# Linear attention and a four-branch feed-forward on one core: batch 1's q and x turned by DMAs instead of by products, with a new order of the first steps

## The chip, the cores and the metric

The kernel runs on one core of one Trainium2 chip. The metric is the device time of one execution in microseconds (us). The profile calls the engines PE (TensorE, matrix products), DVE (VectorE), ACT (ScalarE), POOL (GpSimd) and SP (SyncE, which here only issues transfers).

## The reference

The first half is a linear attention over 8 batches, 8 heads, 576 tokens and head size 64. The second half mixes four two-layer branches over the 4608 resulting rows:

```python
q_p, k_p = phi(q), phi(k)               # phi(x) = max(x + 1, min(exp(x), 1)), in effect
kv  = einsum('bhsd,bhse->bhde', k_p, v);  z = k_p.sum(axis=2)
x   = einsum('bhsd,bhde->bhse', q_p, kv) / (einsum('bhsd,bhd->bhs', q_p, z) + 1e-6)
x   = x as [4608, 512]                  # heads side by side
p   = domain_probs / domain_probs.sum(-1)
out = sum over e of p[:, e] * (relu(x @ w1[e]) @ w2[e])   # w1: 512x1024, w2: 1024x512, 4 branches
```

## The kernel before

**Tiles.** Each batch gives 512 of its 576 tokens to a tile of its own (tiles 0 to 7, in four sub-tiles of 128 tokens, index c); the 64 left rows of all batches form a ninth tile. Heads are worked in four pairs of 128 columns. For every tile and branch the first layer is done by blocks `p1` to `p7` (and `c22`, a step of DVE alone) in two halves d, with seven products of half blocks in place of eight, of four 256-column products each; the second layer by steps `m`, of the same kind, or, for tile 0, by plain steps `y{e}.{ns}{part}`, two 512-column products each, four parts to a sub-tile. The sums of blocks that the seven-product form needs are made by `s` and `t` (of weights, DVE), `ts` (of x, POOL, DVE for tile 0) and `hs` (of the hidden layer, POOL).

**Attention of a batch b** (prefix `b1.`, `b2.` and so on, class `Batch`): loads of k, v and q by quarters; `k`, `q`: ACT writes x + 1 and exp(x); `km`, `qm`: DVE's minimum and maximum of the two; `v`: ACT's cast; `lk`, `lv`, `lq`, `lkm`, `lqm`: the same for the 64 left rows; `kv`: 40 products and two copies by ACT into `kvz`; then q has to be turned, so that its head columns lie on partitions, to be the stationary operand of `nd` (numerators and denominators, followed by DVE's reciprocal and multiplication, `norm`, into x); x has to be turned in its turn to be an operand of the first layer. The left rows go through `qTl`, `nl` and `xl`. q, after its minimum, lies in the tile `qp`, which shares its one buffer with k's `kp`; x shares `vp`'s.

From batch 2 on q and x are turned by DMA transposes issued by SP (`dma_qT` L389, one for the whole of q; `dma_xT` L520, one per pair; `dma_qTl` L397; in `nd_left` L485 for the left rows). Batch 1 alone uses PE: `pe_qT` (L424), `pe_xT` (L508), `pe_qTl` (L405) and `pe_xl` (L414) multiply by an identity into PSUM, from where ACT copies the result.

**The opening** (batch 0, class `First`): loads `lq`, `lk`, `lv` of four parts each and `lpr0` (probabilities); `ke`, `kl`, `km` for k's phi (exp, linear part, minimum), `qe`, `ql`, `qm` for q's, `vc` for v's cast, `kv0` to `kv3` (18 products each and two copies into `kvz`), `qT` (four products and a copy), `nd{g}{hf}` (eight products, then a norm), `xT{pair}{hf}` (two products and a copy), and `L{g}{hf}`, the first layer of branch 0. `LQ`, `LK`, `LV`, `KL`, `QL`, `VC`, `QT`, `KC` and `XT` name the engine that issues or does each (S for SP, A for ACT, P for POOL, V for DVE). `warm` steps are products on zeros.

**The order.** Nothing is scheduled at run time: each engine runs its instructions in the order in which the program emits them, and each waits for what it needs. `CFG["EARLY"]` writes that order out by hand, up to the first branch of tile 2: each mention of a name advances that step by one stage (for `p1.100`, tile 1, branch 0, half 0: the products at the first mention, ACT's copy at the second). What the list leaves over follows by the due times of `ATTN`, `BLK` and the other tables. All weights (`w{layer}{branch}{half}`; branch 0's first layer, `w100` to `w103`, in four quarters) and batch 1's k, v, q (`k0` to `q3`, its left rows `rk`, `rv`) are loaded by POOL's queue, converted to f16 on the way where needed; `b1.load0` to `b1.load5` and `b2.load..` are SP's loads for the batch after. `BANK` says which PSUM buffers a step uses.

```python
for name in " ".join(CFG["EARLY"]).split():
    advance(name)
```

Of the kernel before, what the change touches and what calls it, by code (L numbers as in the profile page):

```python
# [12 lines left out]
FP16 = mybir.dt.float16  # L13
# [33 lines left out]
            xl=95.55,  # L47
# [26 lines left out]
    "LQ": 'SSSS',  # L74
    "LK": 'SSSS',
    "LV": 'SSSS',
    "KL": 'VVVV',
    "VC": 'AAPA',
    "QL": 'VVPV',
    "QT": 'VVAV',  # L80
    "KC": ('VV', 'VA', 'AA', 'AV'),
    "XT": ('AA', 'VV', 'VA', 'VV'),
    "CUT": (((0, 3, 4), (0, 3, 4), (0, 4), (0, 4)), ((0, 2, 4),) * 4),
    "WARM": (14, 5, 3, 1, 2, 1, 1),
    "BANK": {'qT0': 'b', 'qT1': 'py', 'kv2': 'py', 'qT2': 'py', 'kv3': 'b', 'nd10': 'b', 'nd10+': 'py', 'nd00': 'py', 'xT20': 'b', 'nd01': 'b', 'xT00': 'b', 'xT10': 'py', 'xT30': 'py', 'nd11': 'b', 'L20': 'b', 'xT11': 'b', 'L30': 'e', 'L10': 'e', 'L11': 'e', 'L00': 'py', 'L31': 'b', 'L01': 'e', 'L21': 'py', 'b1.lk': 'py', 'b1.q1': 'py', 'b1.q3': 'b', 'b1.q0': 'py', 'b1.nd10': 'b', 'b1.qT0': 'py', 'b1.nd00': 'b', 'b1.xT0': 'b', 'b1.xT3': 'py', 'b1.qTl': 'py', 'b1.nl': 'py'},
# [37 lines left out]
def kernel(  # L123
# [154 lines left out]
    class Batch:  # L278
# [56 lines left out]
        def phi_act(self, name, i):  # L335
# [3 lines left out]
            if name == "q" and self.qp is None:  # L339
                self.qp = pa.tile([P, CM, H, D], FP16, tag="kp", bufs=1, name="qp")  # L340
# [807 lines left out]
```

## Time and profile before

| | |
|---|---|
| median of 3 runs | 491.23 us (491.13 to 491.95) |
| the profiled execution | 491.24 us, of which its span (first to last instruction) is 489.5 us |
| granted TensorE clock, mean | 0.998 |
| PE busy in the span | 477.5 us |
| first product of a first layer (L654) | 18.74 us |
| first product of tile 1 (`p1.10x`) | 66.40 us |
| end of the last weight transfer (`w231`, issued at 68.3) | 76.5 us |

A row of busy time gives for a stage the microseconds in which each engine worked and, in brackets, its instructions; PEld is PE's load of the stationary operand, which runs beside the products. A waits row says which engine and line waited for which, the total, how many times, and the longest. Matrix products overlap, so what one costs is read from the distance between starts, not from its duration. A transfer's landing is counted from the start of its issue.

### The profile page before, as it was taken

To read this page: it belongs to the slowest core of one execution; us is meant where nothing else is said; L and a number is where in the kernel's file an instruction comes from. 1 tells how busy PE (TensorE), PEld (TensorE's weight loads), DVE (VectorE), ACT (ScalarE), POOL (GpSimd) and SP (SyncE) were. 2 spreads that over 40 slices of the span, in tenths; PEclk is the share of its full clock that TensorE was granted. 3 is DMA by queue.
4 is the path that set the end of the run, shared out by engine and by line. 5 is a ranking of instruction groups with operands and counts; after the bars stand their busy time and mean duration, and the time that the engine had idled before them with its cause. 6 is when DMAs were issued, how large, how long until landed. Compare 5 with 4: busy or idle time off the path is not lost.

```text
span 489.5 us, 12007 instructions
## 1 busy us (share of the span) xinstructions
PE 477.5 (98%) x4567; PEld 407.8 (83%) x4567; DVE 382.2 (78%) x801; ACT 330.8 (68%) x656; POOL 358.3 (73%) x341
## 2 busy tenths in 40 slices
PE   7899998999999999999999999999999999999996
PEld 3676665898888988898889888988898888888885
DVE  5768999998958886788769885978687756775686
ACT  5489979855896498748884888478954565446530
POOL 4655044688967896789776976697769877987775
PEclk9999999999999999999999999999999999999999
DMA  8999968532445235524552345423131020002003
GB/s 280 199 226 262 249 127 243 154 94 47 134 154 122 50 112 190 113 60 113 171 128 65 95 144 145 92 56 119 56 76 28 5 95 1 2 0 88 2 1 86
DMA packets 81017, 53.67 MB, mean 110 GB/s; under 512 B 45152, under 2 KB 73696, under 8 KB 80960
## 3 DMA queue, kind: packets, MB, share of 16 engines
q1 hardware_dynamic: 70512, 41.05, 30.7%
q0 software_dynamic: 9888, 11.41, 12.3%
q8 instruction: 35, 0.57, 0.5%
q10 hardware_dynamic: 560, 0.46, 0.3%
q14 instruction: 22, 0.18, 0.1%
HBM read 45.16 MB, written 9.44 MB: 112 GB/s over the span
## 4 chain that ended last, share of the span: by engine, by line
PE 91%; ACT 3%; DVE 2%; DMA 1%; issue 1%; SPq 0%; DVEq 0%; ACTq 0%
PE py L809 39%; PE pb L866 24%; PE pe L866 18%; PE py L714 4%; PE ph L654 1%; PE psum_nd L471 1%; DMA kraws<-in_k_dram 1%; PE psum_kv L443 1%; DVE acc L705 1%; PE pb L809 1%; PE pe L809 0%; DVE t L761 0%; PE psum_nl L489 0%; ACT kp L343 0%; ACT u L877 0%
## 5 line engine op out<-in xcount | busy, mean ns | idle before, releaser
L705 DVE SCALAR_TENSOR_TENSOR acc<-py,p_sb,acc 128x256 f32<-128x256 f32 (+1 forms) x382 | 181.7, 488 | 43.1 <-PE py L809 37.3
L850 DVE CUSTOM_DVE_ANT_0 h<-pe,u 128x512 f16<-128x512 f32 x140 | 96.0, 687 | 46.8 <-PE pe L866 27.1
L866 PEld LDWEIGHTS <-w 128*128 128x128 f16 x1120 | 109.1, 98 | 17.4 <-issue 1.3
L776 POOL TENSOR_TENSOR hs<-h 128x512 f16<-128x512 f16 x64 | 73.9, 1154 | 59.4 <-DVE h L850 57.5
L809 PEld LDWEIGHTS <-h 128*128 128x128 f16 x1024 | 99.6, 98 | 12.7 <-issue 1.2
L809 PE MATMUL py<-w,h 128*128 128x256 f16 x744 | 106.4, 273 | 0.6 <-ACT acc L703 0.6
L877 ACT COPY u<-pb 128x512 f32<-128x512 f32 x140 | 82.5, 592 | 32.4 <-PE pb L866 29.7
L778 POOL TENSOR_TENSOR hs<-hs,h 128x512 f16<-128x512 f16 x64 | 75.0, 1173 | 26.4 <-PE py L809 24.0
L866 PEld LDWEIGHTS <-s 128*128 128x128 f16 x840 | 81.4, 98 | 12.1 <-issue 1.1
L866 PE MATMUL pb<-tt,w 128*128 128x256 f16 x560 | 83.7, 273 | 0.9 <-ACT u L877 0.9
L809 PEld LDWEIGHTS <-hs 128*128 128x128 f16 x768 | 74.4, 98 | 8.9 <-POOL hs L776 0.2
L782 POOL TENSOR_TENSOR hs<-h,hs 128x512 f16<-128x512 f16 x64 | 74.7, 1168 | 0.9 <-PE py L809 0.3
L780 POOL TENSOR_TENSOR h<-h 128x512 f16<-128x512 f16 x64 | 74.8, 1168 | 0.2
L809 PE MATMUL py<-t,hs 128*128 128x256 f16 x496 | 74.3, 273 | 0.0
L899 ACT ACTIVATE h<-pe 128x512 f16<-128x512 f32 x70 | 42.0, 600 | 44.1 <-PE pe L866 40.7
L892 ACT COPY pe<-pb 128x512 f32<-128x512 f32 x70 | 40.1, 574 | 38.6 <-PE pb L866 14.1
L920 ACT ACTIVATE h<-pb 128x512 f16<-128x512 f32 x70 | 42.0, 600 | 7.0 <-PE pb L866 7.0
L866 PE MATMUL pb<-tt,s 128*128 128x256 f16 x280 | 41.8, 272 | 0.6 <-ACT pe L892 0.6
L866 PE MATMUL pe<-tt,s 128*128 128x256 f16 x280 | 41.9, 273 | 0.0
L866 PE MATMUL pe<-xT,s 128*128 128x256 f16 x248 | 37.3, 273 | 0.0
L866 PE MATMUL pe<-xT,w 128*128 128x256 f16 x248 | 37.2, 273 | 0.0
L866 PE MATMUL pb<-xT,w 128*128 128x256 f16 x248 | 37.0, 273 | 0.0
(133 smaller groups left out, 598.7 us busy)
## 6 DMA issues: line engine op xcount, KB each, us to landing
out_dram<-acc SPq DMA_DIRECT2D x32, 256.0 KB, 2.5
w<-in_moe_w_dram POOLq DMA_DIRECT2D x14, 512.0 KB, 10.7
rawb<-in_k_dram SPq DMA_DIRECT2D x24, 256.0 KB, 3.3
rawb<-in_v_dram SPq DMA_DIRECT2D x24, 256.0 KB, 2.8
rawb<-in_q_dram SPq DMA_DIRECT2D x24, 256.0 KB, 2.7
rawq<-in_q_dram SPq DMA_DIRECT2D x4, 256.0 KB, 5.5
w<-in_moe_w_dram POOLq DMA_DIRECT2D x4, 256.0 KB, 6.1
rawb<-in_k_dram POOLq DMA_DIRECT2D x4, 256.0 KB, 8.6
```

What stands on the lines that cost most here:

```text
L705: nc.vector.scalar_tensor_tensor(out=acc, in0=ps, scalar=pscal, in1=acc, op0=AO.mult, op1=AO.add)
L776: nc.gpsimd.tensor_tensor(out=hs[0], in0=a21, in1=a22, op=AO.add)
L778: nc.gpsimd.tensor_tensor(out=hs[1], in0=hs[0], in1=a11, op=AO.subtract)
L780: nc.gpsimd.tensor_tensor(out=a21, in0=a11, in1=a21, op=AO.subtract)
L782: nc.gpsimd.tensor_tensor(out=hs[3], in0=a12, in1=hs[1], op=AO.subtract)
L809: nc.tensor.matmul(out=ps, lhsT=lhsT(k), rhs=rhs[:, k], start=first and k == 0, stop=k == FH - 1, skip_group_check=True,)
L850: nc.vector._custom_dve(TENSOR_ADD_SAT, out=out, in0=ps, in1=u, s0=BIG, s1=0.0)
L866: nc.tensor.matmul(out=ps[:, kk], lhsT=lk(kc), rhs=rhs[:, kc], start=first and kk == 0 and kc == 0, stop=kc == 1, skip_group_check=True,)
L877: nc.scalar.copy(u, self.b)
L892: nc.scalar.copy(self.e5, self.b)
L899: nc.scalar.activation(self.h[:, :, 0, 0:NH], self.e5, AF.Relu)
L920: nc.scalar.activation(self.h[:, :, 1, 0:NH], self.b, AF.Relu)
```

## The change

Batch 1's q is turned by four DMA transposes issued by SP, one for each pair (`b1.qT0` to `b1.qT3`), its x by four (`b1.xT0` to `b1.xT3`), its left rows by two for q and two for x, as in the other batches. The four functions with products go. For this q is laid out pair-major, `[P, NPAIR, CM, P]`, in all batches from 1 on, so that one pair is a contiguous piece. The list `EARLY` is a new order of nearly all steps to the same depth, a few steps longer; the twelve loads of the opening are spread over SP, ACT and POOL, some of the opening's steps change engines, and the products on zeros become 31 in five places instead of 27 in seven. `BANK` gets new entries (not shown). Of `EARLY` the diff shows the stretches of the opening and of batch 1's q and x.

```diff
             xt=(48.15, 50.45, 51.45, 54.8),
             qtl=57.23,
             nl=71.0,
-            xl=95.55,
             next=(-0.5, 0.5, 36.3, 44.55, 46.65, 47.45),
...
-    "LQ": 'SSSS',
-    "LK": 'SSSS',
-    "LV": 'SSSS',
-    "KL": 'VVVV',
-    "VC": 'AAPA',
-    "QL": 'VVPV',
-    "QT": 'VVAV',
-    "KC": ('VV', 'VA', 'AA', 'AV'),
-    "XT": ('AA', 'VV', 'VA', 'VV'),
+    "LQ": 'SSAP',
+    "LK": 'AASS',
+    "LV": 'PSSP',
+    "KL": 'VPVV',
+    "VC": 'AAVA',
+    "QL": 'VVVP',
+    "QT": 'VAAA',
+    "KC": ('AA', 'VA', 'AA', 'VV'),
+    "XT": ('AV', 'AA', 'VV', 'AV'),
     "CUT": (((0, 3, 4), (0, 3, 4), (0, 4), (0, 4)), ((0, 2, 4),) * 4),
-    "WARM": (14, 5, 3, 1, 2, 1, 1),
+    "WARM": (18, 8, 1, 2, 2),
     "EARLY": (
-        "lq0 lk3 lk1 ql0 qe0 lq2 ke1 ql2 kl1 w103 qe2 ke3 kl3 lv1 w100 lk0 lq1 km1 qm0 ke0 kl0 w102 w101 km3 warm0 qT0 ql1 lv0 qm2 km0 vc1 vc0 w111 lq3 ql3 qT0",
-        "warm1 kv1 kv1 lk2 qe3 lv2 vc2 kv1 qT2 qT2 lv3 rk1 kv0 w110 ke2 qe1 kv0 kv0 qm3 vc3 kl2 warm2 nd01 nd00 warm3 qT3 v0 nd00 w200 nd01 warm4 xT10 kv3 xT11",
...
-        "c22.020 b1.k1 p5.021 y1.11 p7.021 p7.021 w131 b1.km1 b1.k0 p4.020 p3.020 y1.20 y1.21 q0 b1.k2 p4.020 p4.021 c22.021 p3.020 b1.load5 p3.021 b1.km0",
-        "y1.12 b1.v3 p4.021 b1.km2 b1.load0 y1.13 b1.kv b1.kv p3.021 y1.22 y1.23 b1.q3 y1.30 y1.13 y1.23 q1 y1.31 y1.32 y1.33 b1.q2 p1.031",
-        "p1.031 y1.00 p1.030 p1.030 b1.qm3 y1.33 b1.qT3 b1.qm2 y1.01 b1.qT2 s3.0 s3.1 p2.030 y1.02 b1.qT3 b1.nd30 y1.03 s3.3 b1.qT2 b1.nd21 b1.loadlq p6.030",
-        "b1.load2 lpr w220 p2.030 b1.nd30 w221 b1.q1 y1.03 p6.030 p5.030 b1.qm1 b1.nd31 p2.031 p7.030 b1.q0 b1.nd31 p6.031 b1.qm0 b1.next y2.00 p7.030 y2.01",
-        "p4.030 p2.031 b1.qT1 p6.031 p4.030 b1.nd21 w230 b1.qT0 b1.nd20 p7.031 c22.030 p5.031 b1.qT0 b1.nd00 b1.xT3 s3.2 b1.nd20 b1.nd01 b1.qT1 p3.030 b1.xT2",
-        "b1.nd00 b1.nd10 b1.nd01 y2.20 b1.xT3 b1.nd11 y2.21 b2.ones p7.031 b1.xT2 b1.lq b1.xT0 y2.22 y2.23 b1.xT0 b1.nd10 b1.nd11 b1.xT1 b1.xT1 b2.load1 y2.02",
...
+        "lk1 lv1 ke1 lq3 qe3 lk3 kl1 kl3 lk0 ql3 lpr0 pr0 qm3 vc1 km1 lv2 lq2 lq0 lv0 ke3 km3 lk2 qe0 lq1 qe1 kl2 warm0 kv1 vc2 lv3 w101 w103 ke2 kl0 ke0 km2",
+        "k0 warm1 kv2 vc0 km0 warm2 kv0 ql1 qm1 kv2 qT1 vc3 ql0 qm0 kv1 kv0 qT1 kv2 kv3 kv1 w100 kv3 qT3 qT0 kv3 nd10 w102 qe2 ql2 qT3 qT0 kv0 warm3 nd00 w110",
+        "nd10 qm2 nd11 qT2 qT2 xT20 w111 nd00 warm4 xT10 xT30 rk0 xT20 xT00 xT10 nd01 nd11 xT30 w200 nd01 xT31 xT21 xT00 L10 L10 xT11 L10 xT21 xT01 xT01 w201",
...
+        "p6.020 y0.33 p2.020 b1.k1 y0.33 p2.021 p7.020 y0.23 b1.km3 s0.2 v2 p5.020 p7.020 w211 y1.10 q2 q1 w130 p6.021 y1.00 p2.021 y1.01 p6.021 p5.021 b1.lv",
+        "p7.021 s2.2 p7.021 b1.lkm b1.v2 c22.020 p3.020 b1.v0 q0 y1.11 c22.021 b1.v3 p4.020 p4.020 b1.km1 b1.q1 y1.02 w131 y1.03 t1.0 b1.kv p4.021 y1.12 p4.021",
+        "y1.13 y1.30 b1.kv p3.021 p1.030 p1.030 y1.31 w220 b1.q2 y1.32 y1.03 y1.20 b1.qm1 b1.q0 p1.031 p1.031 p3.020 y1.21 y1.22 y1.33 y1.13 y1.23 t1.1 p3.021",
+        "q3 b1.qT1 b1.qm2 p2.031 w221 s3.0 s3.1 p2.030 p2.030 y1.33 p6.030 s3.3 p6.031 p6.030 p5.030 p6.031 b1.qm0 b1.nd10 p7.030 p7.030 b1.q3 p7.031 y1.23",
+        "b1.nd10 s3.2 b1.qT2 c22.030 y2.10 p2.031 b1.qT0 y2.20 p4.030 y2.21 b1.qm3 b1.qT3 t0.3 b1.nd21 p3.030 t2.0 b1.nd11 y2.11 b1.nd21 b1.nd11 p5.031 y2.22",
+        "y2.23 y2.12 p7.031 c22.031 b1.nd20 y2.13 p3.031 y2.23 y2.13 b1.nd01 b1.nd00 b1.nd00 y2.00 p4.030 y2.01 y2.02 b1.nd01 b1.nd20 y2.03 y2.30 y2.31 p4.031",
+        "p4.031 b1.nd30 b1.xT1 b1.load1 b1.xT0 y2.03 b1.load0 w230 b1.nd31 b2.k1 y2.32 y2.33 p3.030 b1.xT2 b1.nd31 b1.nd30 b1.xT3 y2.33 b1.loadlq y3.00",
+        "b1.load2 y3.01 t3.0 w231 y3.02 b1.load4 b2.k0 y3.20 y3.03 p3.031 p1.100 y3.03 p1.100 ts1.0 p1.101 p1.101 ts1.1 y3.21 y3.30 t0.1 y3.31 b2.load0 t1.3",
+        "p2.100 p2.101 b2.km0 p2.100 p2.101 b1.lq y3.22 t2.1 b2.load1 p6.100 p6.101 p6.100 p6.101 ts1.2 y3.32 t3.1 t2.3 p5.100 b2.v1 p7.100 p7.100 b2.v0",
+        "b2.ones b2.km1 y3.23 p7.101 b2.v2 c22.100 y3.33 y3.33 p7.101 ts1.3 p4.100 p5.101 b1.load5 p4.100 p3.100 y3.10 b1.load3 p4.101 c22.101 b2.k3 y3.03",
...
@@ -337,9 +336,12 @@
             if name == "k" and self.kp is None:
                 self.kp = pa.tile([P, CM, H, D], FP16, tag="kp", bufs=1, name="kp")
             if name == "q" and self.qp is None:
-                self.qp = pa.tile([P, CM, H, D], FP16, tag="kp", bufs=1, name="qp")
+                self.qp = pa.tile([P, NPAIR, CM, P], FP16, tag="kp", bufs=1, name="qp")
             src = self.raw[name, i]
-            dst = (self.qp if name == "q" else self.kp)[:, :, i * HQ : (i + 1) * HQ, :]
+            if name == "q":
+                dst = self.qp[:, i].rearrange("p c (h d) -> p c h d", h=HQ)
+            else:
+                dst = self.kp[:, :, i * HQ : (i + 1) * HQ, :]
             nc.scalar.activation(dst.rearrange("p c h d -> p h c d"), src, AF.Identity, bias=1.0)
             ee = aps([P, HQ * CM * D], FP32, "psum_ee")
             ee = ee.rearrange("p (c h d) -> p c h d", c=CM, h=HQ)
@@ -386,12 +388,13 @@
                     out=dst, in0=dst, scalar=1.0, in1=el[us], op0=AO.max, op1=AO.min
                 )
 
-        def dma_qT(self):
+        def dma_qT(self, i0=0, n=NPAIR):
             if self.qT is None:
-                self.qT = pa.tile([P, CM, NPAIR, P], FP16, tag="qT", bufs=1, name="qT")
+                self.qT = pa.tile([P, NPAIR, CM, P], FP16, tag="qT", bufs=1, name="qT")
+            pairs = slice(i0, i0 + n)
             nc.sync.dma_start_transpose(
-                out=self.qT.rearrange("p c a i -> p (c a) i"),
-                in_=self.qp.rearrange("p c h d -> p (c h d)"),
+                out=self.qT[:, pairs].rearrange("p a c i -> p (a c) i"),
+                in_=self.qp[:, pairs].rearrange("p a c i -> p (a c i)"),
             )
 
         def dma_qTl(self):
@@ -401,36 +404,6 @@
                     out=self.qTl[:, :, u, us],
                     in_=self.ql[us].rearrange("p h d -> p (h d)"),
                 )
-
-        def pe_qTl(self):
-            ps = aps([P, 2, P], FP16, "psum_ql")
-            for a in range(2):
-                nc.tensor.transpose(out=ps[:, a], in_=self.ql[:, 2 * a : 2 * a + 2], identity=identh)
-            yield
-            for u in range(2):
-                us = slice(u * HP, (u + 1) * HP)
-                nc.scalar.copy(out=self.qTl[:, :, u, us], in_=ps[:, :, us])
-
-        def pe_xl(self):
-            ps = aps([P, 2, P], FP16, "psum_xl")
-            for a in range(2):
-                nc.tensor.transpose(out=ps[:, a], in_=self.xl[:, a], identity=identh)
-            yield
-            c0 = self.b * SL
-            for u in range(2):
-                us = slice(u * HP, (u + 1) * HP)
-                nc.scalar.copy(out=xT_left[:, 2 * u : 2 * u + 2, c0 : c0 + SL], in_=ps[:, :, us])
-
-        def pe_qT(self, pair, eng=nc.vector):
-            ps = aps([P, CM, P], FP16, "psum_qT")
-            for c in range(CM):
-                nc.tensor.transpose(
-                    out=ps[:, c], in_=self.qp[:, c, 2 * pair : 2 * pair + 2], identity=identh
-                )
-            yield
-            if self.qT is None:
-                self.qT = pa.tile([P, CM, NPAIR, P], FP16, tag="qT", bufs=1, name="qT")
-            (eng.copy if eng is nc.scalar else eng.tensor_copy)(out=self.qT[:, :, pair], in_=ps)
 
         def kv(self):
             ps = aps([P, NPAIR, DE], FP32, "psum_kv")
@@ -470,7 +443,7 @@
                 pair, c = divmod(i0 + i, CM)
                 nc.tensor.matmul(
                     out=ps[:, i],
-                    lhsT=self.qT[:, c, pair],
+                    lhsT=self.qT[:, pair, c],
                     rhs=self.kvz[:, pair],
                     start=True,
                     stop=True,
@@ -497,25 +470,13 @@
             self.xl = pa.tile([P, 2, P], FP16, tag="xsl", bufs=1, name="x_sl")
             self.norm(self.xl, ps, 2)
             yield
-            for u in range(2) if self.b != 1 else ():
+            for u in range(2):
                 us = slice(u * HP, (u + 1) * HP)
                 c0 = self.b * SL
                 nc.sync.dma_start_transpose(
                     out=xT_left[:, 2 * u : 2 * u + 2, c0 : c0 + SL],
                     in_=self.xl[us].rearrange("p a i -> p (a i)"),
                 )
-
-        def pe_xT(self, pair):
-            ps = aps([P, CM, P], FP16, "psum_xT")
-            for c in range(CM):
-                nc.tensor.transpose(out=ps[:, c], in_=self.x[:, pair, c], identity=identh)
-            yield
-            if self.xT is None:
-                self.new_xT()
-            nc.scalar.copy(
-                out=self.xT[:, pair],
-                in_=ps.rearrange("p c i -> p (c i)"),
-            )
 
         def dma_xT(self, pair):
             if self.xT is None:
@@ -972,12 +933,12 @@
         if not first:
             put(at["lqd"] + 2, f"b{b}.qTl", bt.dma_qTl)
         if first:
-            put(at["qtl"], f"b{b}.qTl", bt.pe_qTl)
+            put(at["qtl"], f"b{b}.qTl", bt.dma_qTl)
             for i in range(NPAIR):
-                put(at["qt"][i], f"b{b}.qT{i}", bt.pe_qT, i, nc.scalar)
+                put(at["qt"][i], f"b{b}.qT{i}", bt.dma_qT, i, 1)
                 for hf in range(2):
                     put(at["nd"][i], f"b{b}.nd{i}{hf}", bt.nd, i * CM + 2 * hf, 2)
-                put(at["xt"][i], f"b{b}.xT{i}", bt.pe_xT, i)
+                put(at["xt"][i], f"b{b}.xT{i}", bt.dma_xT, i)
             for i in range(NRAW):
                 put(at["next"][i], f"b{b}.load{i}", load, len(mine) + i)
         else:
@@ -985,8 +946,6 @@
             for i in range(6):
                 put(at["nd"][i], f"b{b}.nd{i}", numerators, 3 * i, min(3, NPAIR * CM - 3 * i))
         put(at["nl"], f"b{b}.nl", bt.nd_left)
-        if first:
-            put(at["xl"], f"b{b}.xl", bt.pe_xl)
 
     def warm(n):
 
```

## The prediction

> **What bounds the kernel now.** I read the page's part 1 first, then the busy time by stages, who TensorE (PE) waited for, the queues by tile, and the timeline.
>
> ```profile
> PE 477.5 (98%) x4567; PEld 407.8 (83%) x4567; DVE 382.2 (78%) x801; ACT 330.8 (68%) x656; POOL 358.3 (73%) x341
> ```
>
> PE is the bound on average. The stages say where it is not alone:
>
> ```profile
> core 0: us, PE busy (x) PEld busy (x) DVE busy (x) ACT busy (x) POOL busy (x), PEclk, DMA share, GB/s
> 0.00:15.00 15.00, 11.17 (x90) 5.01 (x91) 9.62 (x24) 8.81 (x14) 8.56 (x18) 1.00 0.94 261
> 50.00:60.00 10.00, 10.00 (x84) 6.73 (x80) 8.82 (x18) 9.47 (x20) 0.00 (x0) 1.00 1.17 255
> 75.00:80.00 5.00, 4.12 (x31) 2.77 (x30) 4.93 (x11) 5.00 (x11) 0.26 (x1) 1.00 0.66 214
> 80.00:85.00 5.00, 4.35 (x65) 2.93 (x64) 4.96 (x8) 4.25 (x9) 4.84 (x4) 1.00 0.85 253
> 100.00:110.00 10.00, 10.00 (x100) 9.01 (x99) 9.39 (x22) 6.27 (x13) 8.20 (x7) 1.00 0.38 91
> ```
>
> To 15 us the loads bind. From 50 to 60, where batch 1's q is turned, PE, VectorE (DVE), ScalarE (ACT) and the DMA engines are all nearly full. From 75 to 85 DVE and ACT are full and PE loses 1.53 us. After that it is PE alone. PE's waits from 20.6 us to 450 us, all of them:
>
> ```profile
> PE pb L866 <- ACT u L877: 0.9, 1, 0.9
> PE pb L866 <- ACT pe L892: 0.6, 1, 0.6
> PE py L809 <- ACT acc L703: 0.6, 1, 0.6
> ```
>
> So 2.1 us is all that a better order can win there; more needs less PE work or an earlier start.
>
> **The products and copies removed.** Two lines of PE's timeline price them:
>
> ```profile
> 54.05 0.39 PE L427 MATMUL psum_qT<-identh,qp 128*128 128x128 f16 x4
> 54.27 0.59 PE L714 MATMUL py<-w,h 128*128 128x512 f16 x2
> ```
>
> Four products hold PE for 54.27 - 54.05 = 0.22 us. Gone are 16 for q, 16 for x, 2 and 2 for the left rows: 36 x 0.055 = 1.98 us, in a stretch where PE is full: **-2.0**. Gone with them are ACT's copies, 4 x 0.60, 4 x 0.585 and 4 x 0.27 = 5.8 us, the last two at 123 us; ACT is not the end of the chain there, but two of PE's three waits (1.5 us) are waits for ACT at 75 to 85 us, a few us behind these copies. DVE is full there as well, so I take 1.0 of the 1.5: **-1.0** (bounds 0 and -1.5).
>
> The pair-major layout of q leaves ACT's and DVE's instructions at the same elements (0.63 and 0.68 us rows): 0. The four more warming products are 4 x 0.21 us in PE's opening idle time (3.8 us to 15 us): 0; without that cover, 0.9.
>
> **The opening.** Before, SP issues all twelve loads, one per 0.5 us; from the fifth on they land every 0.7 us, the last (v, pair 3) at 7.3 + 6.2 = 13.5. That is 288 KB per 0.73 us: rate, not issuing, sets it, so three queues win little. Against it, the new order puts k's pair 1 and q's part 3 on GpSimd (POOL) ahead of the loads of v's pairs 0 and 3. POOL's one such step took 2.14 us. Chain: k1 lands at some 4.2 (the first load took 2.8, its own landing before was 6.5); POOL's k step 2.14 x 576/512 = 2.4, to 6.6; q step to 8.75; issue of v0 0.7, of v3 0.7 from 9.45. Its landing takes between 2.8 (the first load) and 7.1 (w101's, same queue, same crowd); I take 4.3, near the 13.5 by which the same bytes were in before: 13.75. From there to the first layer-1 product: cast, products and kvz copies 1.65; q step and qT copy 0.75; norm of nd10 0.95; qm2 0.35; norm of nd00 0.9; three ACT copies of xT 1.55: 6.2, so 19.95. By then 5.86 us of useful products are done (rows of 0.11 to 0.6 us summed along the new order). Before, the dense stretch starts at 20.64 with 6.74 done. (19.95 - 5.86) - (20.64 - 6.74) = **+0.2**, bounds -1.3 and +3.0 from the landing. ACT's loads of k0 and q2 stand behind its waits for k1 and q3, and are issued at about 6 to 8; k0 then lands at 9.5 to 12, needed by kv0 at 13.4: covered.
>
> **Batch 1 by DMAs.** The transposes that the trace has, all after 86 us:
>
> ```profile
> L523 SPq DMA_TRANSPOSE xT<-x_sb x24: 1188/1216/1380, 105.7 to 366.8; - x24
> ...
> DMA to landing us min/median/max: 2.3/2.3/3.3
> ```
>
> Those are the same 128x512 tiles. But the q ones would now run at 50 to 63 us beside the weight stream. Two rows for that crowd: SP's load of 256 KB issued at 46.23, and the packets between 52 and 60 us:
>
> ```profile
> rawb<-in_k_dram SPq DMA_DIRECT2D x1, 256.0 KB, 7.4
> ```
>
> ```profile
> q0 software_dynamic: 1104, 1.19, 81.7%
> q1 hardware_dynamic: 1105, 0.67, 37.0%
> ```
>
> The two queues got one packet each in turn, 69 pairs per engine in 8 us: 0.116 us a pair. Two stretches with one transpose each (105.5 to 107.4, 109.9 to 112.0 us) show 480 and 651 packets, 35 per engine for each, in 1.2 us of DMA time together: 35 x 0.116 = 4.1 us instead of 0.6 on the engines, so about 2.3 + 3.5 = 5.8 in the crowd. Bounds: 2.3 (alone) and 11.7 (the 256 KB load issued at 49.8 behind others); I take 5.8, as the new order has no loads on SP just ahead of q's.
>
> Whether that is hidden is the distance from issue to use. PE at place x of the new list is at x + 7.45 us (19.95 for place 12.5). b1.kv ends at 48.9; b1.q1 (whose buffer is kp's, so ACT waits there for kv, 2 us, with p4.021's ReLU, kvz and p1.030's copy behind it, none needed before 51) gives 50.0, DVE's minimum 50.7, so qT1 is issued at 50.8 and first used by nd10 at 49.7 + 7.45 = 57.1: 6.3 us. Likewise qT2 5.8, qT0 6.3, qT3 6.3. At 5.8 all are just covered: 0. At 7.4 PE waits 1.1 once (a wait gives the later ones the same time), at 11.7 it waits 5.4.
>
> The Trainium skill (DMA: Bandwidth & Descriptors, Queues, rings and completion order) says each DMA engine takes turns between queue rows packet by packet. The 1104 against 1105 agrees; by the rule alone the sum stays at the covered case, and only the 7.4 row speaks for a wait.
>
> For x the order goes norm, transpose, tile 1's first products. DVE from 50 us has minima, weight sums, accumulations, norms and ReLUs back to back: those from b1.qm1 to b1.nd30's norm sum to 19.5 us at 0.56 to 0.67 each, while PE's list from 50.0 to that place holds 18.0. So DVE ends 1.5 us late, and on the way its ReLU c22.031 is done at 63.7 where p3.031 is due at 63.2, and y2.23's accumulation at 64.4 where y2.00 needs its bank at 63.9, 0.5 each. Between 0.5 and 1.5 I take **+1.2**, bounds 0 (DVE runs ahead in the lighter list before 50 us) and 2.0. After that wait xT0 is issued at 66.4 for p1.100 at 71.4, xT3 at 69.7 for p2.100 at 73.5: 5.0 and 3.9 us, against 2.3 to 3.3 once the weights are in, at 67 to 68 (w230 landed at 46.5 + 17.8 = 64.3 before; w231, issued at 68.3 then, now follows it at once, and y3.02 needs it at 70.1). SP's loads of batch 2 stand between: load1 behind xT1, issued at 64, lands in 3.4 to 7.6; ACT's b2.k1 behind it is at 68.3, so ACT may wait up to 3, with p1.100's copy at 71.8 behind it: covered. The stream itself: the four q and first x transposes hold the DMA engines 5 x 0.6 = 3.0 us, about what SP's loads at 46 to 50 us took in before, now later; w221 then lands at about 61.7, where y2.22 is due at 61.4: 0.3, inside the 1.2 too.
>
> ```profile
> 68.52 3.42 DVE L761 TENSOR_TENSOR t<-w 128x1024 f16<-128x1024 f16 x1
> 69.10 1.17 POOL L847 TENSOR_TENSOR tt<-xT,tt 128x512 f16<-128x512 f16 x1
> 70.22 1.16 POOL L847 TENSOR_TENSOR tt<-xT 128x512 f16<-128x512 f16 x1
> ```
>
> This f16 step takes 0.68 elsewhere; beside POOL's token sums it took 3.42, so 2.7 lost. The new order has five such steps among the four sums, so the loss is there again, 0.68 to 4.6 us of DVE; it is why I don't take all 1.5 above.
>
> **The sum.** -2.0 - 1.0 + 0.2 + 1.2 = -1.6 on the profiled execution's 491.24 (span 489.5 and 1.74 around it, equal to the runs' median of 491.23): 489.6.
>
> **Rivals.** *All hidden*: DVE's lateness falls into slack and ACT's 1.5 is won: -2.0 - 1.5 + 0.2 = 487.9. For it: the 6.3 us distances, and 2.1 us of waits in 430 us now. Against: DVE's 8.82 of 10.
>
> *DVE takes it back*: the change takes nothing from DVE, so PE's 2.0 turns into waits for DVE at 50 to 85 us, +1.2 and 0.8 more, ACT's 1.0 stays lost: 491.24 - 2.0 + 0.2 + 2.0 = 491.4. For it: DVE 4.93 of 5 at 75. Against: its whole load to there is the same in both orders.
>
> The Trainium skill (SBUF — State Buffer, Terms) says of the port pair that DVE and GpSimd share that the loser fully blocks for an instruction. The 3.42 us step agrees, and this rule speaks for that rival.
>
> *Slower, q's transposes starve*: at a landing of over 6.3 us nd10 stands still, PE with it, as no product behind nd10 may pass. At the 9.9 of SP's load issued at 48.9, PE waits 3.6, which includes DVE's 1.2: 491.24 - 2.0 - 1.0 + 0.2 + 3.6 = 492.0; at 11.7 it is 493.8. It decides from 9.1 (a wait of 2.8 undoes the gain). For it: every SP transfer of 46 to 51 us took 7.4 to 14.1. Against: those queued behind each other. I set 492.9.
>
> *Slower, a late opening*: v3 landing after 7.1 instead of 4.3, +2.8: 492.4.
>
> **Numbers.** Forecast 0.33 (489.6), all hidden 0.13, DVE takes it back 0.16, starving 0.25, late opening 0.13. The measurement tells 0.2%, 1.0 us, from no change; so faster 0.46, same 0.16, slower 0.38. The forecast's own range is 488.5 to 490.2; 8 in 10 lie within 487.7 and 493.8.
>
> **What would show it.** Right: no L427, L511, L408, L417 rows; twelve more DMA transposes, q's landing in about 5.8; the first L654 product near 20; PE waits under 1.5 us between 50 and 70 us, put down to DVE, and fewer than 1.5 at 75 to 85. Wrong: PE or its weight load at nd's line waiting for a DMA into qT, L866 waiting for one into xT, L714 for weights, or a first L654 after 21.5.

## The result and the profile after

The changed kernel takes 496.11 us (median of 6 runs, 494.92 to 497.23) against 491.2 us for the kernel before on the same chip (6 runs, 490.71 to 491.95): 1.0099 of its time, 95% interval 1.0082 to 1.0116. It is 4.9 us slower; forecast were 489.6 us, and 487.7 to 493.8 us as the range for 8 in 10. One execution is left out of the times below: in the first run of x alone by DMAs with SP's queue free, one of four took 507.85 us at a granted clock of 0.943, the others 495.74 to 497.61 at 0.986 or more. The profiled execution of after took 496.26 us with a span of 494.5 us, at a granted clock of 1.0.

The first part of the profile's page, of after:

```profile
PE 476.6 (96%) x4535; PEld 406.2 (82%) x4535; DVE 379.1 (77%) x797; ACT 326.9 (66%) x648; POOL 361.1 (73%) x344
```

PE works 0.9 us less (477.5 before) in a span that is 5.0 us longer, so some 5.9 us of new idle time have to be found. The busy time by stages finds them (after, PE alone; the columns are the length of the stage, PE's busy time and instructions, the granted clock, the DMA engines' share and GB/s):

```profile
20.60:50.00 29.40, 29.05 (x256) 1.00 1.19 237
50.00:70.00 20.00, 16.74 (x115) 1.00 1.22 197
70.00:85.00 15.00, 14.83 (x101) 1.00 0.73 186
85.00:130.00 45.00, 40.79 (x404) 1.00 0.54 145
130.00:450.00 320.00, 320.00 (x3144) 1.00 0.34 88
```

The two stages of before that count most here:

```profile
50.00:70.00 20.00, 20.00 (x173) 1.00 0.92 182
85.00:130.00 45.00, 44.98 (x410) 1.00 0.42 110
```

Idle in the five stages is 0.35, 3.26, 0.17, 4.21 and 0 us; before it was 0.12, 0, 1.53, 0.02 and 0.57. So there are two losses: 3.3 us at 50 to 70 us, where batch 1's q is turned, and 4.2 us at 85 to 130 us, well after batch 1's q and x are turned. What ACT cost PE at 70 to 85 us is gone, as hoped. PE's waits of after from 20 to 130 us name those who end the idle time:

```profile
PE psum_nd L444 <- DMA qT<-qp: 4.1, 4, 1.6
PE py L770 <- ACT acc L664: 1.4, 1, 1.4
PE pb L827 <- ACT h L881: 1.0, 1, 1.0
PE pb L827 <- ACT u L838: 0.7, 2, 0.4
PE pb L827 <- POOL tt L808: 0.5, 1, 0.5
```

**The first loss.** Three of the four waits for q (the fourth, 0.9 us, is batch 2's) stand in PE's timeline of after at the numerators of batch 1 (line 444; the bracket is the idle time and what ended it):

```profile
59.95 0.29 PE L444 MATMUL psum_nd<-kvz,qT 128*128 128x130 f16 x2 [1.64 <-DMA qT<-qp]
...
64.29 0.29 PE L444 MATMUL psum_nd<-kvz,qT 128*128 128x130 f16 x2 [1.45 <-DMA qT<-qp]
...
68.44 0.40 PE L444 MATMUL psum_nd<-kvz,qT 128*128 128x130 f16 x4 [0.17 <-DMA qT<-qp]
```

The tile's own view, from 48 to 75 us, gives the issue and the landing of the four transposes:

```profile
L395 SPq DMA_TRANSPOSE qT<-qp x4: 1191/1214/1318, 51.8 to 63.1; - x4
...
DMA to landing us min/median/max: 5.9/8.6/10.1
```

In order they took 8.1, 9.1, 10.1 and 5.9 us; the first three landed at 59.9, 64.2 and 68.4, one every 4.2 us. The packets of after, first from 52.9 to 54.5 us, then from 57 to 59 us:

```profile
q0 software_dynamic: 305, 0.33, 121.3%
```

```profile
q0 software_dynamic: 311, 0.32, 91.3%
q1 hardware_dynamic: 312, 0.08, 29.7%
```

Queue 0 carries the weights, queue 1 the transposes. Between them the landing falls into two parts. The first transpose is issued at 51.8 us, and its first packet leaves only at 55.7, 3.9 us later; until then the weights' queue alone sends. From there the two queues send one packet each in turn, and the transpose's 544 packets, 34 for each of 16 engines, take 3.9 us, to 59.6. In before, the transpose issued at 105.7 us with no weights beside it needed 1.2 us to its first packet (106.9) and 0.8 us for its packets.

**The second loss.** SP's queue of after (start, duration, transfer) issues for 24 of the 26.7 us from 74.6 to 101.3; before it issued for 16 us in that time:

```profile
82.92 0.61 SPq L317 DMA_DIRECT2D rawb<-in_q_dram  x1
83.69 1.35 SPq L295 DMA_DIRECT2D rl<-in_k_dram  x2
...
87.78 2.48 SPq L403 DMA_TRANSPOSE qz<-qlp  x2
...
92.49 0.48 SPq L317 DMA_DIRECT2D rawb<-in_q_dram  x1
93.53 2.44 SPq L476 DMA_TRANSPOSE xT_left<-x_sl  x2
96.10 1.12 SPq L317 DMA_DIRECT2D rawb<-in_q_dram  x1
...
98.26 2.45 SPq L403 DMA_TRANSPOSE qz<-qlp  x2
100.82 0.52 SPq L317 DMA_DIRECT2D rawb<-in_q_dram  x1
```

The four loads of batch 2's q go out at 82.9, 92.5, 96.1 and 100.8 us. Of the added transposes only four stand among them, those of the left rows at 87.8 and 93.5 us, 4.9 us of issuing; the rest is what the new list puts there. In the kernel before they went out between 77.4 and 81.8:

```profile
77.37 2.41 SPq L318 DMA_DIRECT2D rawb<-in_q_dram  x3
...
81.45 0.37 SPq L318 DMA_DIRECT2D rawb<-in_q_dram  x1
```

So ACT of after waits for one of them, PE then waits for ACT (the 1.4 us for line 664 above, which stands behind this step on ACT), and q's transpose of batch 2 is issued at 106.3 instead of 92.7 us and makes PE wait 0.9 us more:

```profile
97.77 0.63 ACT L345 ACTIVATE qp<-rawb 128x512 f16<-128x512 f32 x1 [1.39 <-DMA rawb<-in_q_dram]
```

### The profile page after: what moved, and what is told of

Same layout as the page of the kernel before. It is cut to its first block, busy times and chain, and to the rows that moved or that the text cites. A ratio compares the mean times of both kernels' runs of the same rounds, so it can differ in the third digit from the quotient of the medians.

```text
span 494.5 us, 11962 instructions
## 1 busy us (share of the span) xinstructions
PE 476.6 (96%) x4535; PEld 406.2 (82%) x4535; DVE 379.1 (77%) x797; ACT 326.9 (66%) x648; POOL 361.1 (73%) x344
## 4 chain that ended last, share of the span: by engine, by line
PE 79%; DMA 11%; DVE 4%; ACT 3%; POOL 1%; issue 1%; DVEq 0%; POOLq 0%; ACTq 0%
PE py L770 36%; PE pb L827 21%; PE pe L827 16%; DMA qT<-qp 3%; DMA rl<-in_k_dram 3%; PE py L675 2%; DMA w<-in_moe_w_dram 1%; DMA rawq<-in_q_dram 1%; PE psum_nd L444 1%; DVE acc L666 1%; DMA xT<-x_sb 1%; DMA rawb<-in_q_dram 1%; PE psum_kv L416 1%; DVE t L724 1%; ACT u L838 1%
## 5 line engine op out<-in xcount | busy, mean ns | idle before, releaser
L737 POOL TENSOR_TENSOR hs<-h 128x512 f16<-128x512 f16 x64 | 74.3, 1161 | 55.7 <-DVE h L811 47.9
L739 POOL TENSOR_TENSOR hs<-hs,h 128x512 f16<-128x512 f16 x64 | 73.9, 1155 | 25.4 <-PE py L770 22.9
L770 PEld LDWEIGHTS <-hs 128*128 128x128 f16 x768 | 74.5, 98 | 10.1 <-issue 1.7
L770 PE MATMUL py<-w,hs 128*128 128x256 f16 x248 | 36.9, 273 | 1.4 <-ACT acc L664 1.4
```

Of the source, the lines that this page charges most:

```text
L737: nc.gpsimd.tensor_tensor(out=hs[0], in0=a21, in1=a22, op=AO.add)
L739: nc.gpsimd.tensor_tensor(out=hs[1], in0=hs[0], in1=a11, op=AO.subtract)
L770: nc.tensor.matmul(out=ps, lhsT=lhsT(k), rhs=rhs[:, k], start=first and k == 0, stop=k == FH - 1, skip_group_check=True,)
```

## The experiments

Theories at the start. **A, the crowd**: q's transposes land late because the weights' stream has the DMA engines, and PE waits for them; **B, SP's queue**: the new order and 12 more transposes, 1.2 us of issuing each, hand out batch 2's loads too late. Their rival **C**: one loss is the other's lateness handed on, or the new order as such is slower. All ratios are to the kernel before on the same chip.

### Without q's transposes

```diff
 def dma_qT(self, i0=0, n=NPAIR):
+    if self.b == 1:
+        self.qT = self.qp
+        return
     nc.sync.dma_start_transpose(...)
```

> The new kernel without the four DMA transposes of batch 1's q: the numerators read q as it lies (that part of the computation is left out), so they wait only for DVE's minimum. All else, the order too, as in the new kernel. Theory (the transposes land late beside the weight stream, 8 to 10 us in the profile, and PE waits 1.64 + 1.45 + 0.17 us for them): PE's idle time from 50 to 70 us falls from 3.26 us to under 0.6; the waits of 85 to 160 us (4.0 us, ACT waiting for batch 2's q) come from the order of SP's loads and stay: 492.5 to 493.5. Rival one, the later waits only follow from the first: both go, 489.5 to 490.5. Rival two, the new order itself makes PE wait there (DVE, PSUM buffers): 495 to 496.5.

492.61 us (9 runs), ratio 1.0030 (1.0010 to 1.0050), so 3.4 us of the 4.9 went with four transposes. PE's stages:

```profile
50.00:70.00 20.00, 20.00 (x173) 1.00 0.93 177
70.00:85.00 15.00, 14.70 (x100) 1.00 0.78 205
85.00:130.00 45.00, 41.00 (x410) 1.00 0.54 137
```

The first loss is 0 and the second is still 4.0 us: it is not the first one handed on. PE is busy all of 50 to 70 us as well, so DVE's lateness, for which the prediction charged 1.2 us, costs nothing once q is there.

### One q load earlier

```diff
-... p4.110 b2.load6 p1.120 ... t3.3 b2.load4 b2.q2 ...
+... p4.110 b2.load4 p1.120 ... t3.3 b2.load6 b2.q2 ...
```

> The new kernel with two loads of SP exchanged in the list: batch 2's third quarter of q (b2.load4), which stood one step ahead of its use on ACT, takes the place of batch 3's first k (b2.load6), a dozen steps earlier. If the later loss comes from that load's place in the order: ACT's wait of 1.4 us at that quarter and PE's 1.36 us at 98 us go, with part of the 2.4 us of 110 to 160 us behind it: 493.0 to 494.8. If those waits only follow from the first loss at 58 to 68 us: 495.8 to 496.5.

496.24 us (4 runs), 1.0106 (1.0070 to 1.0143): nothing won. That time fits the second expectation, though its reason, lateness handed on from the first loss, is out by the run before. The wait at 98 us went (idle at 90 to 100 us 0.07 instead of 1.46), and came back at 100 to 120 us (2.3 instead of 0.9): the last q load now went out at 102.2 us. So one place in the queue is not the bound; whether the q loads together are is tested below.

### Half of the weight stream of 50 to 70 us left out

In both kernels, the second layer's weights of branches 2 and 3 are zeroed by POOL instead of loaded.

```diff
-            nc.gpsimd.dma_start(out=w2_sb[e][:, fs], in_=w2_src[e, :, fs])
+            if e >= 2:
+                nc.gpsimd.memset(w2_sb[e][:, fs], 0.0)
+            else:
+                nc.gpsimd.dma_start(out=w2_sb[e][:, fs], in_=w2_src[e, :, fs])
```

> The new kernel with the second-layer weights of branches 2 and 3 set to zero by GpSimd in place of their four transfers of 1 MB (read) each: that part of the computation is left out, the DMA engines have no crowd from some 50 us on. To be set against the kernel before with the same edit. If the crowd makes the transposes late: they land in 2.3 to 3.5 us, PE waits under 0.5 us at the numerators from 50 to 70 us, and this kernel is at most 1.8 us above the other (the later loss stays), or 1 to 2 us below it if the later loss follows from the first. If the transposes are slow for another reason (their small packets, the SP queue): landing stays over 6 us and the difference stays at 4 to 5 us.

> The kernel before with the same edit (second-layer weights of branches 2 and 3 zeroed by GpSimd, four transfers fewer), as the other half of the pair. It has no transposes in that stretch: 490 to 492, within 1 us of the kernel before by every theory, unless weights or GpSimd's work bound it there.

After: 492.15 us (10 runs), 1.0029 (1.0012 to 1.0045). Before: 490.22 us (10 runs), 0.9978 (0.9965 to 0.9992). The difference between the two kernels falls from 0.0099 to 0.0051, which is 2.5 us still (1.9 by the medians), a little over the 1.8 us expected. The transfers of the edited after from 50 to 70 us:

```profile
qT<-qp SPq DMA_TRANSPOSE x4, 2.4
```

Same place, same instructions: 2.4 us instead of 8.6, and PE idles 0 at 50 to 70 us. The first transpose, issued at 52.6 us, sends its first packet at 53.9, after 1.3 us and not 3.9. Theory A stands. The 4.2 us of the second loss are still there (40.80 busy of 45).

### Copies instead of transposes

```diff
+    if self.b == 1:
+        nc.sync.dma_start(out=self.qT[:, pairs], in_=self.qp[:, pairs])
+        return
     nc.sync.dma_start_transpose(...)
```

> The kernel after with batch 1's four q transposes replaced by plain copies of the same 128 KB from the same tile to the same tile in SP's queue (1 KB packets where the transposes move 256 byte ones; q arrives unturned, so the result is not the reference's). Theory P (packets): a transpose is late because each of its many small packets waits for its turn beside the weights' packets; a copy with a quarter of the packets lands in 3 to 5 us, PE doesn't wait for it, and the time is 492 to 493.5 us. Rival (the crowd alone): any transfer that starts there waits for the weight stream; it lands in 8 to 10 us as the transposes do, and the time stays at 495.5 to 497 us.

493.8 us (8 runs), 1.0054 (1.0038 to 1.0070), a little over what the packets' theory gave. The transfers from 50 to 70 us:

```profile
qT<-qp SPq DMA_DIRECT2D x4, 128.0 KB, 5.6
```

Same bytes, same crowd: 5.3 to 5.7 us, with no queueing, and PE idles 0 at 50 to 70 us. The start is as late as the transposes': the first copy is issued at 52.2 us, and from there to 56.0 the weights' queue sent 713 packets and SP's none. Then the copy's 144 packets, 9 for each engine, took 1.5 us, where the first transpose's 34 took 3.9. So the late start of 3.8 to 3.9 us meets both forms, and the transpose's many small packets cost 2.4 us more, which also makes the next one queue behind it.

### Two queues

```diff
+            eng = nc.scalar if self.b == 1 and i0 in (0, 2) else nc.sync
-            nc.sync.dma_start_transpose(
+            eng.dma_start_transpose(
```

> The kernel after, with two of batch 1's four q transposes (pairs 0 and 2) issued in ACT's DMA queue and two in SP's, as before in place and size. Theory Q (one queue's turn): the four transposes queue behind one another, 4.2 us of service each beside the weight stream, so two queues serve them side by side; PE's waits for q fall from 3.3 us to 0.5 to 1.5 us, and the time to 493.5 to 495 us (ACT loses two issues, 1.2 us each, off the critical path at that place). Rival (the engines' rate): the small packets share the DMA engines whatever queue they stand in; landings stay at 8 to 10 us, and the time at 495.5 to 497 us.

499.72 us (4 runs), 1.0174 (1.0159 to 1.0189): outside what either expected, and no test of them. The timeline of ACT's two issues:

```profile
61.24 1.29 ACTq L396 DMA_TRANSPOSE qT<-qp  x1
...
69.43 1.21 ACTq L396 DMA_TRANSPOSE qT<-qp  x1
```

SP's two were issued at 52.5 and 66.9. Each was issued only after the one before it, in the other queue, had landed (the first at 60.4), so they ran one at a time, and ACT stood still for 7.44 us around the last. Whether two queues would serve them side by side stays open.

### Batch 2's q loads first

```diff
-b2.load6 ... b3.load1 ... b2.load4 ... b2.load3 ... b2.load8 ... b2.load5
+b2.load4 ... b2.load3 ... b2.load5 ... b2.load6 ... b3.load1 ... b2.load8
```

> The kernel after, with six loads of the raw ring in another order in SP's list: the three late q loads of batch 2 (issued at 92.5, 96.1 and 100.8 us in the profile of after) take the first three of six places (91.5 to 101.4 us), the k and v loads that stood there take the last three. Theory A (the order): SP hands out the q loads too late for batch 2's q steps, and PE's 4 us of idle between 85 and 130 us follow from it; the last q load then goes out some 7 us sooner, and the time is 492.5 to 494.5 us, PE idle in 85 to 130 us below 2 us. Theory B (the slots): the ring has six slots, a load can't start before the load six ahead of it has been used, so a new order only moves the lateness to k and v; 495.5 to 497 us, idle still 3.5 us or more.

> The kernel after with both suspected causes taken away: batch 1's four q transposes left out (the numerators read q as it lies, so that the result is not the reference's), and the six ring loads with batch 2's q loads first. Two separate losses, both as named: 488.5 to 490.5 us (the kernel with q unturned took 492.6, less 2 to 4 us). If the order of the loads is not the cause of the later loss: 492 to 493.5 us as before this edit. PE idle in 50 to 70 us 0 in either case.

The order alone: 494.78 us (4 runs), 1.0066 (1.0047 to 1.0084). With q unturned: 491.68 us (10 runs), 1.0004 (0.9993 to 1.0015). Against the same kernels in the old order that is 1.6 and 1.3 us less, with PE idle at 85 to 130 us 2.0 and 2.2 us instead of 4.2 and 4.0. The first and then the second kernel:

```profile
85.00:130.00 45.00, 42.96 (x430) 1.00 0.53 140
```

```profile
85.00:130.00 45.00, 42.78 (x429) 1.00 0.52 141
```

That is just over what theory B gave (494.5 us at most, idle under 2 us), and well under the rival's 3.5 us or more of idle time: B is right for half of the second loss. (The profiled execution of the order alone, 492.89 us, is the fastest of its four.) The last q load now went out 9 us sooner, at 91.4 us instead of 100.8, but batch 2's q transpose only 2.5 us sooner, at 103.8: 12 us behind that load, where it was 5.5 us in after, so something else than the loads' issue holds it there. In the second kernel the other half is waits of 1.1 us for batch 2's q transpose, 0.6 for POOL and 0.4 for ACT; no run takes them apart. I had expected 488.5 to 490.5 us with both causes gone; 491.68 is the kernel before's own time, and the gain of the prediction's sum isn't there.

### x alone by DMAs, in the order of before; and all of it

```diff
-                put(at["xt"][i], f"b{b}.xT{i}", bt.pe_xT, i)
+                put(at["xt"][i], f"b{b}.xT{i}", bt.dma_xT, i)
...
-            put(at["qtl"], f"b{b}.qTl", bt.pe_qTl)
+            put(at["qtl"], f"b{b}.qTl", bt.dma_qTl)
```

> The kernel before with only batch 1's x, left x and left q rows turned by DMAs (20 products and their copies on ACT fewer); q turned by products as before, the opening and the list of steps as before but for the dropped second halves of these steps. If the later loss of after lies in the list's order and not in these DMAs: 488 to 490.5 us, with PE's 1.5 us of idle at 70 to 85 us gone. If the DMAs themselves cost it (SP's 13 us of added issues push batch 2's loads): 492 to 495 us, with PE idle at 90 to 130 us as in after.

> The kernel before with all of batch 1's turns by DMAs, q by head pairs, in the order and the opening of before (only the left rows of batch 2 are loaded after batch 1's left q has been read, since that load would stand ahead of two q transposes in SP's queue and wait for it). If the landing in the crowd is the first loss: the first numerators stand closer behind their transposes here (3 to 7 us) than in after, so PE waits 4 to 9 us at 50 to 70 us and the time is 493.5 to 498 us. If the new order is what makes after slower: 489 to 491.5 us.

x alone: 498.89 us (4 runs), 1.0157 (1.0133 to 1.0180). All by DMAs: 506.07 us (4 runs), 1.0311 (1.0287 to 1.0335), over even the expected range of theory A. So the new order doesn't make these DMAs dear: in the old one they cost three times as much (15.1 us against 4.9). What the new order costs or wins with products for q and x no run shows. SP and PE of the x kernel:

```profile
52.19 7.24 SPq L250 DMA_DIRECT2D praw<-in_moe_domain_probs_dram  x2
64.83 1.25 SPq L294 DMA_DIRECT2D rl<-in_k_dram  x2
...
68.82 5.24 SPq L521 DMA_TRANSPOSE xT<-x_sb  x4
```

```profile
73.98 0.37 PE L864 MATMUL pb<-xT,w 128*128 128x256 f16 x1 [6.66 <-DMA xT<-x_sb]
```

The transposes land in 2.3 us, but stand in SP's queue behind two loads of 4 KB that took 7.24 us to issue in the crowd and behind the left rows, which wait 5.1 us for ACT. Behind PE's long wait the granted clock was 0.50 from 74 to 78 us, so a part of this run's cost is the clock. From 85 to 130 us this kernel idles only 0.5 us, with eight more transposes in SP's queue than before, so these alone don't make the second loss. (The wait of 7.5 us ahead of it gave the loads time, so this is no clean proof.)

### The numerators later

```diff
-b1.nd10 p7.030 p7.030 b1.q3 p7.031 y1.23 ... t0.3 b1.nd21 p3.030 t2.0 b1.nd11 y2.11 ... y2.22 ...
+p7.030 p7.030 b1.q3 p7.031 y1.23 b1.nd10 ... t0.3 p3.030 t2.0 y2.11 ... y2.22 b1.nd21 b1.nd11 ...
-p1.100 ... p1.101 ... y3.21 y3.30
+y3.21 y3.30 p1.100 ... p1.101
```

> The kernel after with batch 1's numerator steps some 2 to 3 us of PE work later in the list (behind parts of the first tile's second layer that stood after them) and tile 1's first two steps behind four more such parts; the transposes are left as and where they are. If the first loss is only the distance between a transpose's issue and its use (landings of 8 to 10 us against 6 us in the list): PE's waits for q fall from 3.3 us to below 1 us, and the time to 493 to 495 us. If the chain behind the numerators (x, its transposes, tile 1) needs them at the old places: the wait reappears as one for xT at 70 to 80 us, and the time stays at 495.5 to 497.5 us.

> The same with the six ring loads of batch 2 in the order q first, as in the run of that order alone. If the two losses are separate, as the runs with q unturned say: 1.3 to 2 us under the run with the numerators later alone, so 491.5 to 493.5 us; the kernel before at 491.2 us is reached at best, not beaten by more than 1 us. If the second loss is only the first one's lateness handed on: no difference between the two runs.

496.11 us (4 runs), 1.0094 (1.0068 to 1.0121), and with the q loads first 494.95 us (4 runs), 1.0071 (1.0045 to 1.0096). The second is 1.1 us under the first, a little less than the 1.3 to 2 expected, and over its range of 491.5 to 493.5 us. The larger waits of the first, 20 to 130 us:

```profile
PE psum_nd L444 <- DMA qT<-qp: 1.9, 3, 1.1
PE py L770 <- ACT acc L664: 1.8, 2, 1.5
PE pb L827 <- ACT u L838: 1.7, 2, 1.6
PE py L675 <- DVE acc L666: 0.9, 2, 0.6
```

The waits for batch 1's q fell to 0.85 us, as the distance theory had it, but the time stayed, as the other had it, though not by a wait for x: 1.5 us came back as waits for DVE, 0.4 as waits for ACT, and PE's idle time from 20.6 to 130 us is 7.8 us instead of 8.0. Here moved steps only handed the lateness on.

### x alone by DMAs, with SP's queue free

q by products; SP's left rows and second probabilities behind x's transposes.

```diff
-b1.load2 lpr w220 ... b1.next y2.00 ... b1.xT1 b2.load1
+b1.load2 w220 ... y2.00 ... b1.xT1 b1.next b2.load1 ... b1.load3 lpr
```

> The kernel before with batch 1's x and left rows turned by DMAs, q by products, and SP's loads of batch 2's left rows and of the second probabilities moved behind the four x transposes (the steps that read the left rows a little later too); tile 1's first steps where they were. x's transposes then go out at 62 to 66 us and land 2.3 us later, the last near 68, while tile 1's first product is due at 65 to 66: a wait of 2 to 3 us instead of 7.5. If the x part is worth its 20 products and copies (-1.1 and up to -1.5): 490.5 to 493 us. If SP's later work is pushed into a new wait at 70 to 130 us: 494 us or more.

> The same with tile 1's first steps some 2.5 us of second-layer products later, so that x has landed. If the x part is worth its 20 products and copies: 488.5 to 490.5 us, under the kernel before. If the time freed is lost to SP's later work or to DVE: 491 to 494 us.

496.23 us (3 runs), 1.0109 (1.0075 to 1.0144), and 495.63 us (4 runs), 1.0102 (1.0046 to 1.0157). The first fits its expectation of 494 us or more; the second is over both of its own. The wait for x is gone in the second, and nothing is lost at 90 to 130 us; two others are there, and the second of them costs more than its length:

```profile
70.65 0.60 PE L864 MATMUL pb<-tt,s 128*128 128x256 f16 x4 [1.75 <-POOL tt L845]
...
79.37 0.60 PE L487 MATMUL psum_nl<-kvz,qz 128*128 128x130 f16 x4 [2.48 <-DMA qz<-qlp]
79.81 1.60 PE L712 MATMUL py<-w,h 128*128 128x512 f16 x4
```

```profile
80.00:82.00 2.00, 2.00 (x8) 0.53 0.53 53
82.00:84.00 2.00, 2.00 (x12) 0.62 0.77 220
```

A last run moved these two steps as well:

```diff
-y2.13 b1.nl y3.22 ... c22.100 b1.nl y3.23 ... b2.load9 b1.nl p4.100
+y2.13 y3.22 ... y3.10 b1.nl y3.00 y3.01 b1.nl p4.101 y3.02 b1.nl
```

> The kernel of the last run with batch 1's left numerators and norms some 5 us of products later, and tile 1's first step that reads the token sums some 2 us later. If those two waits and the clock behind them are what is left: 489.5 to 492 us, PE idle at 60 to 90 us below 1.5 us and its clock 1.0 there. If the list is so tight that the waits only move on: 493 us or more.

496.81 us (4 runs), 1.0108 (1.0080 to 1.0137). The waits moved on again: 3.09 us for DVE at 82.9, 1.41 for weights at 76.6, 1.09 for DVE at 84.4. No kernel tried here that does all of the work beats the one before.

## Why the prediction was wrong, step by step

- **The landing in the crowd, 5.8 us**, is the term that failed first. It measured 8.1 us for the first transpose, with nothing of its own queue ahead of it. The sharing that the sum added was right: 35 packets at 0.116 us a pair are 4.1 us, and 34 took 3.9 here. The Trainium skill (DMA: Bandwidth & Descriptors, Queues, rings and completion order) says that the engine takes turns packet by packet; this trace agrees where both queues have packets, with 311 to 312. What failed is the rest of the 2.3 us, which the sum kept as measured alone: the start, from the issue to the first packet, was 1.2 us there and 3.9 beside the weights. 3.9 for the start, 3.9 for the packets and the 0.3 that is left of the 2.3 make 8.1. The trace of before had it: SP's load issued at 46.23 us sent nothing until 49.8, so 3.6 of its 7.4 us were start, but the sum read that row as one number and set it aside. That the weights' stream causes the late start is shown by the run without it (1.3 us); how it holds the first packet back is not.
- **"A wait gives the later ones the same time"** failed too. It looked at each transpose alone. The first three are issued 3.3 us apart and served one every 4.2 us, so the second and third queued behind the one before, landed still later (9.1 and 10.1), and the distances of 5.8 to 6.3 us were short by more each time. PE's waits for it: 1.64 + 1.45 + 0.17 = 3.26, where the sum had 0. The rival *q's transposes starve* named mechanism, place and price: a wait of 3.6 at a landing of 9.9; without the idle time of the next point the account below comes to 492.1 us, against its 492.0.
- **SP's loads behind x's transposes, "covered"**: this looked at one load, `load1` at 64 us, and stopped at 72 us. Nothing in the sum followed the queue to 101 us, where the four q loads of batch 2 were up to 19 us later than before. Cost: 4.2 us of idle time at 85 to 130 us; the order of six loads is shown to be half of it, the cause of the rest stays open.
- **ACT relief, -1.0** (bounds 0 and -1.5): idle at 70 to 85 us fell from 1.53 to 0.17, and to 0.30 in the run without q's transposes, where PE had not stood before. The size fits; whether ACT's copies or the new order won it, no run separates.
- **Products, -2.0**: PE's busy time fell by 0.86 us in all. Four more warming products, charged at 0 in idle time, take back part of it (their row grew from 9.6 to 10.0 us); the rest I can't place, since kernels with the same products differ by over 1 us in this sum (476.07 to 477.78 at a granted clock of 0.996 or more). No run showed the 2.0 in its time.
- **The opening, +0.2**: the first layer's first product was forecast at 19.95 and stands at 20.13. The term is right, partly by two errors that cancel: v's last load was issued at 10.11 us, not 9.45, and landed in 3.3 us, not 4.3. Idle time at 20.6 to 50 us grew by 0.23.

```profile
20.13 1.03 PE L615 MATMUL ph<-xT,w 128*128 128x256 f16 x8
```

- **DVE late, +1.2** (bounds 0 and 2.0): 0 in the run without q's transposes. The rival *DVE takes it back* is out with it.

Sum over the span: -0.86 busy, and idle +0.23 (20.6 to 50), +3.26, -1.36, +4.19, -0.57 (130 to 450) and +0.13 (behind 450) make +5.0, which is 494.5 - 489.5. Where the gain went: 1.4 us of waits at 70 to 85 us and 0.9 us of PE's work were won, and then paid for with 7.5 us: 3.3 for q's late transposes, and 4.2 of which SP's order of loads is shown to be half.

## What to carry to other kernels

Turning by DMA takes work from the engine that is the bound and gives it to two queues, so price the queues: split a landing into the time to its first packet and the time of its packets, measure both beside the streams that will run there, and count the service time of several transfers in a row, not the landing of one alone. Follow the issuing engine's queue until it has caught up, tens of microseconds behind the edit, since each added issue delays every load behind it. In a list where several engines are nearly full, a step that is moved to hide one wait can just move that wait, as it did in the last runs here.

## What the runs showed of the hardware

- 128 KB from SBUF to SBUF by a DMA transpose took 2.4 us without a weight stream beside it and 8.1 to 10.1 us beside one; as a plain copy in the same crowd it took 5.3 to 5.7 us.
- Beside the weight stream a transfer issued by SP sent its first packet 3.6 to 3.9 us after its issue (a load at 46.23 us in before, the first transpose in after, the first copy in the run with copies); without it, 1.2 to 1.3 us. After that the queues took turns one to one, 0.114 us a pair.
- Two loads of 4 KB took 7.24 us to issue on SP in the crowd of the run with x alone by DMAs (2.4 us at 80 us in after): there the issuing engine itself was held up, and all behind it.
- A wait of PE can cost more than its length. Behind 2.48 us of idle time the granted clock was 0.53 and 0.62 for 4 us, and four products of 128x512 took 1.60 us instead of 1.03; behind the waits of 1.64 and 1.45 us of after, and the 1.75 us above, it stayed at 1.00. The Trainium skill (TensorE: Matmul & The Clock Gate, Part 1: The HAM clock gate) gives about 3.4 us of idle time for this; here less was enough.
